# Transposed attention with paired 64-row score tiles, the mixer of one batch laid between the attention groups of the next, and transposes by DMA

## The chip, the cores and the metric

The kernel runs on one NeuronCore of a Trainium2 chip. Five engines work side by side, each through its own instructions in order: TensorE (PE in the profile; its weight loads have a row of their own, PEld), VectorE (DVE), ScalarE (ACT), GpSimd (POOL) and SyncE (SP). POOL and SP here mostly issue DMA transfers; those that change the type from float32 to bfloat16 are issued by POOL, stores by SP. TensorE writes to PSUM, eight banks of 512 float32 per partition; DVE and ACT read it.

The metric is the device time of one execution in microseconds. Lower is better.

## What is computed

The inputs `u` and `v` are 8 x 3008 x 256, `z` is 8 x 3008 x 64, all float32. For each of the 8 batches:

```python
scores = (z @ z.T) / 3008                     # 3008 x 3008
attn   = maximum(scores, 0) ** 2
x      = u * (attn @ v)                       # 3008 x 256, gated attention
h      = maximum(x.T @ w_tok1, 0) @ w_tok2    # token layers: 3008 -> 256 -> 3008
y      = x + h.T
h2     = maximum(y @ w_ch1, 0) @ w_ch2        # channel layers: 256 -> 1536 -> 256
out    = y + h2
```

The scores are symmetric, so a tile of them can serve as its own transpose. There is no softmax: squares of the positive scores multiply `v` directly.

## The kernel before

All matmuls take bfloat16 operands. The 3008 rows are cut into 24 tiles of 128 (the last holds 64 rows and is padded with zeros). The batches run one after another, and each goes through these stages.

**z transposes.** 24 tiles of `z` are transposed on TensorE (line 125) and copied by ACT to `z_T` (line 126), 64 partitions by 3072.

**Attention.** Queries are taken in six groups of 512 columns. For each of the 24 key tiles, one matmul with 64 contraction rows gives the scores of 128 keys by 512 queries (line 143). ACT applies relu and the scale (line 150), DVE squares (line 153), and four matmuls use the four 128-column pieces of the square as weights and the 256 columns of `v` as the moving operand (line 156), which accumulate the output with queries on partitions. Two PSUM banks hold the four accumulators. At the end of a query group DVE multiplies by `u` (line 165), which gives `x_sb` with rows on partitions.

**Token layers.** The first accumulates over the 24 row tiles into one bank (line 173), ACT applies relu (line 182); the second makes one 128 x 256 tile per row tile (line 187), which DVE adds to `x_sb` (line 193).

**Transposes.** The channel layers need `x_sb` with channels on partitions: 48 transposes of 128 x 128 on TensorE (line 199), copied by ACT and DVE in turn (lines 203 and 205).

**Channel layers.** For each 512 rows, twelve pairs of matmuls give the 1536 hidden channels (line 215); relu alternates between ACT and DVE (lines 222 and 224). Then each 128 rows take twelve matmuls of 256 columns (line 230), DVE adds `x_sb` (line 237), and SP stores the rows.

The order on each engine is made by the framework's scheduler from the order of the code and the free buffers: six PSUM buffers are shared by all tiles but the accumulators, and six work buffers hold relus and squares. It runs up to six score matmuls ahead of the matmuls that use them. POOL issues the loads of the next batch while one is worked on.

Of the kernel before, what the change touches and what calls it, by code (L numbers as in the profile page):

```python
# [8 lines left out]
F32 = mybir.dt.float32  # L10
BF16 = mybir.dt.bfloat16
AX = mybir.AluOpType
ACT = mybir.ActivationFunctionType


@with_exitstack
def kernel(
# [16 lines left out]

    P = 128
    KT = (S + P - 1) // P
    Sp = KT * P
    assert D == 256
    assert d_tok == 256
    assert d_ch % P == 0  # L40
    CHT = d_ch // P
    DT = D // P

    Q_SUB = 4
    QG = (KT + Q_SUB - 1) // Q_SUB
    Q_W = Q_SUB * P

# [3 lines left out]
    inbuf = ctx.enter_context(tc.tile_pool(name="inbuf", bufs=2))  # L51
    work = ctx.enter_context(tc.tile_pool(name="work", bufs=6))
    big = ctx.enter_context(tc.tile_pool(name="big", bufs=1))
    psum = ctx.enter_context(tc.tile_pool(name="psum", bufs=6, space=bass.MemoryType.PSUM))
    psum_acc = ctx.enter_context(tc.tile_pool(name="psum_acc", bufs=1, space=bass.MemoryType.PSUM))

    ident = consts.tile([P, P], BF16)
    make_identity(nc, ident)

    def load_sbuf_SD(ap_src, name):  # L60
        t = inbuf.tile([P, KT, D], BF16, tag=name, name=name)
        nc.gpsimd.memset(t[:, KT - 1, :], 0.0)
        nc.gpsimd.dma_start(
            out=t[:, : KT - 1, :],
            in_=ap_src[: (KT - 1) * P, :].rearrange("(t p) d -> p t d", p=P),
        )
        nc.gpsimd.dma_start(
            out=t[: S - (KT - 1) * P, KT - 1, :],
            in_=ap_src[(KT - 1) * P :, :],
        )  # L70
        return t

    def load_batch(b):
        z_sb = inbuf.tile([P, KT, d_qk], BF16, tag="z_sb")
        nc.gpsimd.memset(z_sb[:, KT - 1, :], 0.0)
        nc.gpsimd.dma_start(
            out=z_sb[:, : KT - 1, :],
            in_=z[b, : (KT - 1) * P, :].rearrange("(t p) d -> p t d", p=P),
        )
        nc.gpsimd.dma_start(  # L80
            out=z_sb[: S - (KT - 1) * P, KT - 1, :],
            in_=z[b, (KT - 1) * P :, :],
        )
        v_sb = load_sbuf_SD(v[b], "v_sb")
        u_sb = load_sbuf_SD(u[b], "u_sb")
        return z_sb, v_sb, u_sb

    next_data = load_batch(0)

    w_tok1_sb = consts.tile([P, KT, d_tok], BF16)  # L90
    nc.gpsimd.memset(w_tok1_sb[:, KT - 1, :], 0.0)
    nc.gpsimd.dma_start(
        out=w_tok1_sb[:, : KT - 1, :],
        in_=moe_w_tok1[: (KT - 1) * P, :].rearrange("(t p) d -> p t d", p=P),
    )
    nc.gpsimd.dma_start(
        out=w_tok1_sb[: S - (KT - 1) * P, KT - 1, :],
        in_=moe_w_tok1[(KT - 1) * P :, :],
    )

    w_tok2_sb = consts.tile([P, DT, Sp], BF16)
    nc.gpsimd.memset(w_tok2_sb[:, :, S:], 0.0)
    nc.gpsimd.dma_start(
        out=w_tok2_sb[:, :, :S],
        in_=moe_w_tok2.rearrange("(tc t) s -> t tc s", t=P),
    )

    w_ch1_sb = consts.tile([P, DT, d_ch], BF16)
    nc.gpsimd.dma_start(
        out=w_ch1_sb[:],  # L110
        in_=moe_w_ch1.rearrange("(dc d) c -> d dc c", d=P),
    )

    w_ch2_sb = consts.tile([P, CHT, D], BF16)
    nc.gpsimd.dma_start(
        out=w_ch2_sb[:],
        in_=moe_w_ch2.rearrange("(cc c) d -> c cc d", c=P),
    )

    for b in range(B):  # L120
        z_sb, v_sb, u_sb = next_data
        z_T = inbuf.tile([d_qk, Sp], BF16, tag="z_T")
        for k in range(KT):
            zt_ps = psum.tile([d_qk, P], BF16, tag="ps", name="zt_ps")
            nc.tensor.transpose(zt_ps[:], z_sb[:, k, :], ident)  # L125
            nc.scalar.copy(z_T[:, k * P:(k + 1) * P], zt_ps[:])  # L126
        if b + 1 < B:
            next_data = load_batch(b + 1)

        x_sb = big.tile([P, KT, D], BF16, tag="x_sb")  # L130

        for qg in range(QG):
            q0 = qg * Q_SUB
            n_q = min(Q_SUB, KT - q0)
            out_bank = [
                psum_acc.tile([P, 2, D], F32, tag=f"acc{i}", name=f"out_bank{i}")
                for i in range((n_q + 1) // 2)
            ]
            out_ps = [out_bank[i // 2][:, i % 2, :] for i in range(n_q)]
            qslice = slice(q0 * P, q0 * P + n_q * P)  # L140
            for k in range(KT):
                sc_ps = psum.tile([P, Q_W], F32, tag="ps", name="sc_ps")
                nc.tensor.matmul(  # L143
                    sc_ps[:, : n_q * P],
                    z_T[:, k * P : (k + 1) * P],
                    z_T[:, qslice],
                    start=True, stop=True,
                )
                relu_sb = work.tile([P, Q_W], BF16, tag="relu_sb")
                nc.scalar.activation(relu_sb[:, : n_q * P], sc_ps[:, : n_q * P],  # L150
                                     ACT.Relu, scale=inv_S)
                attn_sb = work.tile([P, Q_W], BF16, tag="attn_sb")
                nc.vector.tensor_mul(attn_sb[:, : n_q * P], relu_sb[:, : n_q * P],  # L153
                                     relu_sb[:, : n_q * P])
                for qi in range(n_q):
                    nc.tensor.matmul(  # L156
                        out_ps[qi][:],
                        attn_sb[:, qi * P : (qi + 1) * P],
                        v_sb[:, k, :],
                        start=(k == 0 and qi % 2 == 0),  # L160
                        stop=(k == KT - 1),
                        skip_group_check=True,
                    )
            for qi in range(n_q):
                nc.vector.tensor_mul(  # L165
                    x_sb[:, q0 + qi, :], u_sb[:, q0 + qi, :], out_ps[qi][:]
                )

        a_bank = psum_acc.tile([P, 2, D], F32, tag="acc0", name="a_bank")
        a_ps = [a_bank[:, i, :] for i in range(DT)]  # L170
        for k in range(KT):
            for tc_ in range(DT):
                nc.tensor.matmul(  # L173
                    a_ps[tc_][:],
                    w_tok1_sb[:, k, tc_ * P:(tc_ + 1) * P],
                    x_sb[:, k, :],
                    start=(k == 0 and tc_ == 0), stop=(k == KT - 1),
                    skip_group_check=True,
                )
        a_relu = work.tile([P, DT, D], BF16, tag="a_relu")  # L180
        for tc_ in range(DT):
            nc.scalar.activation(a_relu[:, tc_, :], a_ps[tc_][:], ACT.Relu)  # L182

        for k in range(KT):
            h_ps = psum.tile([P, D], F32, tag="ps", name="h_ps")
            for tc_ in range(DT):
                nc.tensor.matmul(  # L187
                    h_ps[:],
                    w_tok2_sb[:, tc_, k * P:(k + 1) * P],
                    a_relu[:, tc_, :],  # L190
                    start=(tc_ == 0), stop=(tc_ == DT - 1),
                )
            nc.vector.tensor_add(x_sb[:, k, :], x_sb[:, k, :], h_ps[:])  # L193

        u2T_all = big.tile([P, DT, Sp], BF16, tag="u2T_all")
        for k in range(KT):
            for dc in range(DT):
                t_ps = psum.tile([P, P], BF16, tag="ps", name="t_ps")
                nc.tensor.transpose(  # L199
                    t_ps[:], x_sb[:, k, dc * P:(dc + 1) * P], ident  # L200
                )
                if (k * DT + dc) % 2 == 0:
                    nc.scalar.copy(u2T_all[:, dc, k * P:(k + 1) * P], t_ps[:])  # L203
                else:
                    nc.vector.tensor_copy(u2T_all[:, dc, k * P:(k + 1) * P], t_ps[:])
        for sg in range(QG):
            s0 = sg * Q_SUB
            n_s = min(Q_SUB, KT - s0)
            SW = n_s * P
            u2T = u2T_all[:, :, s0 * P: s0 * P + SW]  # L210
            h2pre = big.tile([P, CHT, Q_W], BF16, tag="h2pre", bufs=2)
            for cc in range(CHT):
                hp = psum.tile([P, Q_W], F32, tag="ps", name="hp")
                for dc in range(DT):
                    nc.tensor.matmul(  # L215
                        hp[:, :SW],
                        w_ch1_sb[:, dc, cc * P:(cc + 1) * P],
                        u2T[:, dc, :],
                        start=(dc == 0), stop=(dc == DT - 1),
                    )  # L220
# [50 lines left out]
```

## Time and profile before

| | |
|---|---|
| runs | 1598.85 us median of 3 (1594.77 to 1600.70) |
| profiled execution, first to last instruction | 1595.4 us |
| median of the runs less that span | 3.45 us |
| TensorE matmul busy | 1539.8 us, 97% |
| DVE busy | 915.5 us, 57% |
| ACT busy | 837.8 us, 53% |
| POOL busy | 60.5 us, 4% |
| mean granted TensorE clock | 0.977 |

The profile comes from one execution. Its own time is given by the span from the first to the last instruction; the runs are timed from outside, without a profile. A row of a group reads: line, engine, operation, output and input tiles, shapes, count, then busy time and mean duration in ns, then the idle time of the engine just before these instructions and what ended it. A row of a stretch reads: from and to, length, then for each engine its busy time and number of instructions, then granted clock (1.00 is full), DMA share and GB/s. A row of the timeline reads: start, duration, engine, line, operation and the number of instructions merged in it. A row of a DMA issue ends with KB and the us from issue to landing.

The ends of matmuls are modelled by the profiler, and a matmul's duration contains its latency, so the pace of matmuls is read from one start to the next.

### The profile page before, as it was taken

Reading aid. Unit: us, or ns where it says so; the run is one execution under the profiler, and the core shown is the slowest. Engines: PE = TensorE matmul, PEld = TensorE weight load, DVE = VectorE, ACT = ScalarE, POOL = GpSimd, SP = SyncE. Lnnn points to the kernel's source line nnn. Section 1 sums busy time; section 2 is a strip of 40 time slices with the busy share of each in tenths; the row PEclk is TensorE's granted clock in tenths of the full one; section 3 lists DMA queues with packets and bytes.
Section 4 is the critical chain, followed back from the end, with each engine's and each line's share of the span. In section 5 each row is a group of like instructions: output and inputs, shape, how many; then the busy total and the mean of one; then the engine's idle time right before and its main releaser. Section 6 shows DMA issues by size and latency. Waiting matters only on the chain.

```text
span 1595.4 us, 27271 instructions
## 1 busy us (share of the span) xinstructions
PE 1539.8 (97%) x10512; PEld 954.0 (60%) x10560; DVE 915.5 (57%) x2208; ACT 837.8 (53%) x1841; POOL 60.5 (4%) x85
## 2 busy tenths in 40 slices
PE   7999999999999999999999999999999999999999
PEld 4556655566555665556655566555665556655566
DVE  3566555565565555556556565565655646556465
ACT  5663366633666336653367533775337743376442
POOL 4001000010000000010000100001000000000000
PEclk9999999999999899999999999999999999999999
DMA  9906110061100611006110051101510000100001
GB/s 176 126 1 91 54 22 1 1 92 54 23 1 1 95 50 23 1 6 93 48 21 1 10 92 50 17 1 18 88 50 3 1 1 27 52 1 1 1 28 52
DMA packets 105362, 58.77 MB, mean 37 GB/s; under 512 B 27984, under 2 KB 104720, under 8 KB 105232
## 3 DMA queue, kind: packets, MB, share of 16 engines
q0 software_dynamic: 78096, 32.38, 16.4%
q1 hardware_dynamic: 27136, 24.65, 4.6%
q8 instruction: 82, 1.34, 0.3%
q14 instruction: 48, 0.39, 0.1%
HBM read 64.75 MB, written 24.64 MB: 56 GB/s over the span
## 4 chain that ended last, share of the span: by engine, by line
PE 81%; ACT 8%; DVE 8%; issue 2%; DMA 1%; POOL 0%; POOLq 0%
PE out_bank L156 36%; PE op L230 16%; PE hp L215 16%; PE sc_ps L143 7%; ACT relu_sb L150 6%; DVE attn_sb L153 4%; PE a_bank L173 3%; DVE x_sb L193 3%; PE t_ps L199 3%; ACT z_T L126 2%; DMA v_sb<-in_v_dram 1%; ACT u2T_all L203 1%; DVE x_sb L165 0%; PE h_ps L187 0%; ACT a_relu L182 0%
## 5 line engine op out<-in xcount | busy, mean ns | idle before, releaser
L150 ACT ACTIVATE relu_sb<-sc_ps 128x512 bf16<-128x512 f32 x1152 | 582.6, 629 | 273.7 <-PE sc_ps L143 273.6
L153 DVE TENSOR_TENSOR attn_sb<-relu_sb 128x512 bf16<-128x512 bf16 x1152 | 466.1, 424 | 377.1 <-ACT relu_sb L150 333.2
L156 PE MATMUL out_bank<-v_sb,attn_sb 128*128 128x256 bf16 x4608 | 579.0, 275 | 20.1 <-DVE attn_sb L153 9.2
L156 PEld LDWEIGHTS <-attn_sb 128*128 128x128 bf16 x4608 | 387.7, 98 | 253.0 <-DVE attn_sb L153 180.6
L222 ACT ACTIVATE h2pre<-hp 128x512 bf16<-128x512 f32 x288 | 171.9, 597 | 290.8 <-DVE res L237 178.1
L143 PE MATMUL sc_ps<-z_T 64*128 64x512 bf16 x1152 | 295.3, 380 | 0.0
L230 PE MATMUL op<-w_ch_sb,h2pre 128*128 128x256 bf16 x2304 | 259.4, 273 | 0.0
L215 PE MATMUL hp<-u2T_all,w_ch_sb 128*128 128x512 bf16 x1104 | 251.0, 382 | 3.7 <-issue 1.5
L230 PEld LDWEIGHTS <-h2pre 128*128 128x128 bf16 x2304 | 225.5, 98 | 36.3
L224 DVE TENSOR_SCALAR h2pre<-hp 128x512 bf16<-128x512 f32 x288 | 199.3, 692 | 68.2 <-PE hp L215 65.0
L215 PEld LDWEIGHTS <-w_ch_sb 128*128 128x128 bf16 x1152 | 113.8, 99 | 128.9 <-issue 5.8
L143 PEld LDWEIGHTS <-z_T 64*128 64x128 bf16 x1152 | 91.3, 94 | 136.8 <-issue 55.7
L237 DVE TENSOR_TENSOR res<-op,x_sb 128x256 f32<-128x256 f32 x192 | 81.6, 425 | 157.1 <-PE op L230 157.1
L193 DVE TENSOR_TENSOR x_sb<-x_sb,h_ps 128x256 bf16<-128x256 bf16 x192 | 64.3, 415 | 56.7 <-PE h_ps L187 56.7
L203 ACT COPY u2T_all<-t_ps 128x128 bf16<-128x128 bf16 x192 | 46.3, 267 | 74.6 <-PE t_ps L199 69.4
L165 DVE TENSOR_TENSOR x_sb<-u_sb,out_bank 128x256 bf16<-128x256 bf16 x192 | 67.9, 416 | 3.9 <-PE out_bank L156 3.9
L199 PE MATMUL t_ps<-ident,x_sb 128*128 128x128 bf16 x384 | 53.1, 273 | 11.5 <-ACT u2T_all L203 9.3
L187 PE MATMUL h_ps<-a_relu,w_tok_sb 128*128 128x256 bf16 x384 | 56.9, 270 | 3.8 <-ACT a_relu L182 3.8
L173 PE MATMUL a_bank<-x_sb,w_tok_sb 128*128 128x256 bf16 x384 | 52.7, 307 | 5.0 <-DVE x_sb L165 5.0
L126 ACT COPY z_T<-zt_ps 64x128 bf16<-64x128 bf16 x192 | 32.1, 319 | 42.4 <-PE zt_ps L125 42.4
L199 PEld LDWEIGHTS <-x_sb 128*128 128x128 bf16 x384 | 38.1, 120 | 26.2 <-issue 21.4
L173 PEld LDWEIGHTS <-w_tok_sb 128*128 128x128 bf16 x384 | 42.3, 110 | 15.4 <-issue 6.4
(28 smaller groups left out, 193.4 us busy)
## 6 DMA issues: line engine op xcount, KB each, us to landing
out_dram<-res SPq DMA_DIRECT2D x184, 128.0 KB, 1.7
v_sb<-in_v_dram POOLq DMA_DIRECT2D x8, 1472.0 KB, 12.5
u_sb<-in_u_dram POOLq DMA_DIRECT2D x8, 1472.0 KB, 18.0
z_sb<-in_z_dram POOLq DMA_DIRECT2D x8, 368.0 KB, 6.0
w_ch_sb<-in_moe_w_ch_dram POOLq DMA_DIRECT2D x2, 768.0 KB, 30.9
w_tok_sb<-in_moe_w_tok_dram POOLq DMA_DIRECT2D x1, 1504.0 KB, 28.1
w_tok_sb<-in_moe_w_tok_dram POOLq DMA_DIRECT2D x1, 1472.0 KB, 23.0
out_dram<-res SPq DMA_DIRECT2D x8, 64.0 KB, 1.9
```

The source lines that it names most:

```text
L143: nc.tensor.matmul(sc_ps[:, : n_q * P], z_T[:, k * P : (k + 1) * P], z_T[:, qslice], start=True, stop=True,)
L150: nc.scalar.activation(relu_sb[:, : n_q * P], sc_ps[:, : n_q * P], ACT.Relu, scale=inv_S)
L153: nc.vector.tensor_mul(attn_sb[:, : n_q * P], relu_sb[:, : n_q * P], relu_sb[:, : n_q * P])
L156: nc.tensor.matmul(out_ps[qi][:], attn_sb[:, qi * P : (qi + 1) * P], v_sb[:, k, :], start=(k == 0 and qi % 2 == 0), stop=(k == KT - 1), sk ...
L173: nc.tensor.matmul(a_ps[tc_][:], w_tok1_sb[:, k, tc_ * P:(tc_ + 1) * P], x_sb[:, k, :], start=(k == 0 and tc_ == 0), stop=(k == KT - 1), s ...
L193: nc.vector.tensor_add(x_sb[:, k, :], x_sb[:, k, :], h_ps[:])
L199: nc.tensor.transpose(t_ps[:], x_sb[:, k, dc * P:(dc + 1) * P], ident)
L215: nc.tensor.matmul(hp[:, :SW], w_ch1_sb[:, dc, cc * P:(cc + 1) * P], u2T[:, dc, :], start=(dc == 0), stop=(dc == DT - 1),)
L222: nc.scalar.activation(h2pre[:, cc, :SW], hp[:, :SW], ACT.Relu)
L224: nc.vector.tensor_single_scalar(h2pre[:, cc, :SW], hp[:, :SW], 0.0, AX.max)
L230: nc.tensor.matmul(op[:], h2pre[:, cc, si * P:(si + 1) * P], w_ch2_sb[:, cc, :], start=(cc == 0), stop=(cc == CHT - 1),)
L237: nc.vector.tensor_add(res[:], op[:], x_sb[:, k, :])
```

## The change

The kernel is written anew around the same mathematics; nothing of the computation is left out.

- **Transposed attention.** `v` is now the weight operand and the square of the scores is the moving operand, so the attention output has channels on partitions: per key tile two matmuls of 512 columns instead of four of 256. The gate multiplies by a transposed `u`, and gives `xT`.
- **Paired scores.** `z` is loaded twice side by side, so that its transpose has the 64 rows on partitions 0 to 63 and again on 64 to 127. Two key tiles form a pair, one on each half of the rows, each into its own PSUM bank; one relu and one square serve both (1024 columns). Four key tiles form a group, six groups a strip of 512 queries, 36 groups a batch; the sixth strip is 448 wide, without padding. The last key tile, with 64 rows, is split over the halves in the same way.
- **DMA transposes.** `z`, `u`, the gated `xT` and `xT` after the token layers are transposed by DMA, issued by SP, instead of on TensorE.
- **Order by hand.** The order of the code is the order on each engine. The scores of a group, with their relus and squares, are issued one group ahead. The mixer (token and channel layers) of a batch is cut into pieces with a cost and an earliest group; after each key tile of the next batch's attention a running budget takes pieces from the queue. What is left after the last group runs at the end. A planner by accumulated load chooses ACT or DVE for the relus of the first channel layer.
- **PSUM.** Scores: two buffers of two banks; the accumulator: one buffer of two banks; all of the mixer: two buffers of one bank.

```diff
+    def load_z(b):
+        zr = sb.tile([P, KT, 2, d_qk], BF16, tag="zr", name="zr", bufs=1)
+        for h in range(2):
+            nc.gpsimd.dma_start(
+                out=zr[:, : KT - 1, h, :],
+                in_=z[b, : (KT - 1) * P, :].rearrange("(t p) d -> p t d", p=P))
...
+        zT = sb.tile([P, KT, P], BF16, tag="zT", name="zT", bufs=2)
+        nc.sync.dma_start_transpose(out=zT[:], in_=zr.rearrange("p t h d -> p (t h d)"))
...
+    def scores(n):
...
+        for pr in range(GK // 2):
+            sc = psum.tile([P, 2, QW], F32, tag="sc", name="sc", bufs=2)
+            for r in range(2):
+                k = g * GK + pr * 2 + r
+                h = slice(r * d_qk, (r + 1) * d_qk)
                 nc.tensor.matmul(
+                    sc[:, r, :W], zT[h, k * P:(k + 1) * P], zT[h, q * QW:q * QW + W],
+                    start=True, stop=True)
+            pss.append(sc)
+        for sc in pss:
+            rl = sb.tile([P, 2, QW], BF16, tag="rl", name="rl", bufs=3)
+            nc.scalar.activation(rl[:, :, :W], sc[:, :, :W], ACT.Relu, scale=inv_S)
+            at = sb.tile([P, 2, QW], BF16, tag="at", name="at", bufs=5)
+            nc.vector.tensor_mul(at[:, :, :W], rl[:, :, :W], rl[:, :, :W])
...
+    def av(n):
...
+            accs[b, q] = psum.tile([P, DT, QW], F32, tag="acc", name="acc", bufs=1)
...
+                nc.tensor.matmul(
+                    acc[:, dh, :W], vt[rows, k, dh * P:(dh + 1) * P], at[rows],
+                    start=(k == 0), stop=(g == NG - 1 and last), skip_group_check=True)
...
+    def gate(b, q):
...
+        x = sb.tile([P, DT, QW // P, P], BF16, tag="x", name="x_sb", bufs=7)
+        nc.sync.dma_start_transpose(
+            out=x.rearrange("p h t d -> p (h t) d"), in_=xT.rearrange("p h s -> p (h s)"))
...
+    def relu_out(dst, src, n):
+        if load["ACT"] + 0.1 + n / 1200 <= load["DVE"] + 0.15 + n / 960:
+            load["ACT"] += 0.1 + n / 1200
+            nc.scalar.activation(dst, src, ACT.Relu)
+        else:
+            load["DVE"] += 0.15 + n / 960
+            nc.vector.tensor_single_scalar(dst, src, 0.0, AX.max)
...
+        def tok2(q, dh):
...
+            h = psum.tile([P, QW], F32, tag="mm", name="h_ps", bufs=2)
...
+            nc.vector.tensor_add(xT[:, dh, :W], xT[:, dh, :W], h[:, :W])
...
+        def ch1(q, cc):
...
+            hp = psum.tile([P, QW], F32, tag="mm", name="hp", bufs=2)
...
+        def ch2(q, half):
+            op = psum.tile([P, 2, D], F32, tag="mm", name="op", bufs=2)
...
+            res = sb.tile([P, 2, D], F32, tag="res", name="res", bufs=3)
...
+            head.append(Work(0.87, g0, lambda q=q: tok1(q)))
...
+                head.append(Work(0.43, g0 + 4, lambda q=q, dh=dh: tok2(q, dh)))
+        c1 = [[Work(0.43, g0 + 6, lambda q=q, cc=cc: ch1(q, cc)) for cc in range(CHT)]
+              for q in range(NQ)]
+        c2 = [[Work(2.7, g0 + 6, lambda q=q, hf=hf: ch2(q, hf)) for hf in range(2)]
+              for q in range(NQ)]
...
+    share = per_batch / (NQ * NG)
...
+    for n in range(N):
...
+        if n + 1 < N:
+            scores(n + 1)
+        if b >= 1:
+            budget += share
+        thunks = av(n)
+        for j, t in enumerate(thunks):
+            t()
+            if j == GK - 1 and g == NG - 1:
+                gate(b, q)
+            want = budget * (GK - 1 - j) / GK
+            while budget > want:
+                i = next((i for i, w in enumerate(queue) if w.earliest <= n), None)
...
+                w.fn()
+                budget -= w.cost
+        if q == NQ - 1 and g == NG - 1:
+            head, tail = mixer(b, n + 3)
+            queue = head + queue + tail
+    for w in queue:
+        w.fn()
```

More of the change, by code (lines that the diff above doesn't have):

```diff
@@ new lines, in load_v @@
+    def load_v(b, parts):
+        vt = sb.tile([P, KT, D], BF16, tag="v", name="v_sb", bufs=2)
+        step = (KT - 1 + parts - 1) // parts
+        for t0 in range(0, KT - 1, step):
+            t1 = min(t0 + step, KT - 1)
+            nc.gpsimd.dma_start(
+                out=vt[:, t0:t1, :],
+                in_=v[b, t0 * P:t1 * P, :].rearrange("(t p) d -> p t d", p=P))
+        for r in range(2):
+            nc.gpsimd.dma_start(
+                out=vt[r * TAIL:(r + 1) * TAIL, KT - 1, :], in_=v[b, (KT - 1) * P:, :])
+        return vt
@@ L120 @@
[L120 to L186, printed above, removed]
-                nc.tensor.matmul(
[L188 to L220, printed above, removed]
-                if cc % 2 == 0:
-                    nc.scalar.activation(h2pre[:, cc, :SW], hp[:, :SW], ACT.Relu)
-                else:
-                    nc.vector.tensor_single_scalar(h2pre[:, cc, :SW], hp[:, :SW],
-                                                   0.0, AX.max)
-            for si in range(n_s):
-                k = s0 + si
-                op = psum.tile([P, D], F32, tag="ps", name="op")
@@ new lines, in av, with one @@
+    def av(n):
+        b, q, g = groups[n]
+        W = widths[q]
+        if g == 0:
+            accs[b, q] = psum.tile([P, DT, QW], F32, tag="acc", name="acc", bufs=1)
+        acc = accs[b, q]
+        tiles = attn.pop(n)
+        vt = vs[b]
+        order = list(range(GK))
+        if g == NG - 1:
+            order = [GK - 1] + order[:-1]
+        def one(i, last):
+            k = g * GK + i
+            at = tiles[i // 2][:, i % 2, :W]
+            for dh in range(DT):
+                rows = slice(0, P)
+                if k == KT - 1:
+                    rows = slice(dh * TAIL, (dh + 1) * TAIL)
+                nc.tensor.matmul(
+                    acc[:, dh, :W], vt[rows, k, dh * P:(dh + 1) * P], at[rows],
+                    start=(k == 0), stop=(g == NG - 1 and last), skip_group_check=True)
+        return [lambda i=i, j=j: one(i, j == GK - 1) for j, i in enumerate(order)]
@@ new lines, in ch2 @@
+            load["DVE"] += 0.7
+        for q in range(NQ):
+            head.append(Work(0.87, g0, lambda q=q: tok1(q)))
+        for q in range(NQ):
+            for dh in range(DT):
+                head.append(Work(0.43, g0 + 4, lambda q=q, dh=dh: tok2(q, dh)))
[3 more added lines that the diff above has]
+              for q in range(NQ)]
@@ new lines, in mixer @@
+        tail += c1[0]
+        for q in range(NQ):
+            nxt = c1[q + 1] if q + 1 < NQ else []
+            half = len(nxt) // 2
+            tail += nxt[:half] + [c2[q][0]] + nxt[half:] + [c2[q][1]]
+        return head, tail
+    zTs[0] = load_z(0)
+    vs[0] = load_v(0, 4)
+    uTs[0, 0] = load_uT(0, 0)
+    load_weights()
+    uTs[0, 1] = load_uT(0, 1)
+    queue = []
+    per_batch = 0.87 * NQ + 0.43 * NQ * DT + 0.43 * CHT * NQ + 2.7 * 2 * NQ
+    share = per_batch / (NQ * NG)
+    budget = 0.0
```

230 lines of the change are left out of this document (155 added, 75 removed).

## The prediction, made before the change was run

> **What bounds the kernel now.** I read the page's engine shares and its chain of waits first, then the stretches of one batch (the second, from 211.19 us on), then the groups of instructions by shape, then single rows of the timeline.
>
> ```profile
> span 1595.4 us, 27271 instructions
> PE 1539.8 (97%) x10512; PEld 954.0 (60%) x10560; DVE 915.5 (57%) x2208; ACT 837.8 (53%) x1841; POOL 60.5 (4%) x85
> PE 81%; ACT 8%; DVE 8%; issue 2%; DMA 1%; POOL 0%; POOLq 0%
> ```
>
> TensorE is busy 97% of the span and carries 81% of the chain; ACT and DVE are half idle. The next view gives busy time by stage: attention, token layer 1, token layer 2, the transposes, the channel layers, the z transposes of the next batch.
>
> ```profile
> 211.19:319.95 108.76, 105.69 (x721) 59.69 (x721) 65.76 (x167) 73.39 (x149) 2.79 (x5) 1.00 0.06 5
> 319.95:325.82 5.87, 5.40 (x48) 4.69 (x48) 0.61 (x2) 0.43 (x2) 4.07 (x5) 1.00 0.78 98
> 325.82:332.89 7.07, 7.07 (x48) 4.62 (x48) 6.43 (x20) 0.23 (x1) 0.00 (x0) 1.00 1.42 193
> 332.89:340.78 7.89, 6.47 (x50) 4.77 (x48) 6.13 (x27) 5.41 (x23) 0.00 (x0) 0.66 1.09 148
> 340.78:404.09 63.31, 62.83 (x429) 42.38 (x433) 35.14 (x62) 21.91 (x38) 0.00 (x0) 0.99 0.14 46
> 404.09:407.61 3.52, 3.40 (x25) 2.25 (x25) 0.42 (x1) 3.24 (x21) 0.00 (x0) 1.00 0.20 60
> ```
>
> One batch is 196.4 us. To see whether "busy" is really full, I take the pace from starts: 23 channel matmuls of 512 columns, 48 of 256, and so on; then an attention stretch with short runs of each kind.
>
> ```profile
> 352.11 5.13 PE L215 MATMUL hp<-u2T_all,w_ch_sb 128*128 128x512 bf16 x23
> 357.07 5.40 PE L230 MATMUL op<-w_ch_sb,h2pre 128*128 128x256 bf16 x48
> 362.53 0.38 PE L215 MATMUL hp<-u2T_all,w_ch_sb 128*128 128x512 bf16 x1
> ...
> 70.20 0.61 PE L156 MATMUL out_bank<-v_sb,attn_sb 128*128 128x256 bf16 x4
> 70.74 1.03 PE L143 MATMUL sc_ps<-z_T 64*128 64x512 bf16 x4
> 71.71 0.39 PE L156 MATMUL out_bank<-v_sb,attn_sb 128*128 128x256 bf16 x2
> ```
>
> (357.07 - 352.11)/23 = 0.2157 us for 512 columns. From 357.07 to 362.53 are 5.46 us: 48 of 256 columns and one 512 whose record is missing (23 of 24), so (5.46 - 0.216)/48 = 0.1092 us. A 64-row score costs the same as a 128-row matmul. Each change between 64-row and 128-row work costs 0.10: 0.54 - 4 x 0.1092 = 0.103, and 0.97 - 4 x 0.2157 = 0.107. By these prices the attention of a batch is 144 x (0.2157 + 4 x 0.1092) = 94.0; the other 14.8 of 108.8 are changes and waits for the score chain.
>
> **The change, part by part.** Every step is costed on TensorE, then I look for what makes it wait. "Group" is four key tiles of one 512-query strip; 36 groups make a batch.
>
> *Attention matmuls.* A group has two score pairs (0.431 if the two halves of a pair run at once), eight attention-times-V matmuls of 512 columns (1.726) and two changes (0.20): 2.36 us. 36 groups are 85.0; the sixth strip is 448 wide, less 6 x 2.157/8 = 1.6: 83.4. Nothing in the trace shows two 64-row matmuls on different rows. The bounds for a pair are 0.2157 (both at once) and 0.431 (one after another); I take the first, because the two use different rows and different PSUM banks, and the nearest row, a full 128-row matmul, streams exactly those rows in 0.2157. The other end adds 36 x 2 x 0.2157 x 8, less a 48th, = 122 us.
>
> [...]
>
> *Removed on TensorE.* z transposes (3.5) and the transposes before the channel layers (7.9) go to DMA. Padding 3072 to 3008 is in the strip width above.
>
> *Mixer matmuls.* Token 1: 48 x 0.1092 = 5.2. Token 2, now 24 of 512: 5.2. Channel 1: 144 x 0.2157 = 31.1. Channel 2: 288 x 0.1092 = 31.4. Less 0.8 for the narrow strip: 72.2 a batch.
>
> Now the waits. ACT and DVE serve the new, longer tiles at these prices:
>
> ```profile
> L150 ACT ACTIVATE relu_sb<-sc_ps 128x512 bf16<-128x512 f32 x1152 | 582.6, 629 | 273.7 <-PE sc_ps L143 273.6
> L153 DVE TENSOR_TENSOR attn_sb<-relu_sb 128x512 bf16<-128x512 bf16 x1152 | 466.1, 424 | 377.1 <-ACT relu_sb L150 333.2 <-PE out_bank L156 2.5
> L224 DVE TENSOR_SCALAR h2pre<-hp 128x512 bf16<-128x512 f32 x288 | 199.3, 692 | 68.2 <-PE hp L215 65.0
> L222 ACT ACTIVATE h2pre<-hp 128x512 bf16<-128x512 f32 x288 | 171.9, 597 | 290.8 <-DVE res L237 178.1 <-PE hp L215 107.6 <-PE t_ps L199 5.1
> L165 DVE TENSOR_TENSOR x_sb<-u_sb,out_bank 128x256 bf16<-128x256 bf16 x192 | 67.9, 416 | 3.9 <-PE out_bank L156 3.9
> L182 ACT ACTIVATE a_relu<-a_bank 128x256 bf16<-128x256 f32 x16 | 5.3, 381 | 67.0 <-PE a_bank L173 67.0
> ...
> 909.58 0.39 PE L143 MATMUL sc_ps<-z_T 64*128 64x512 bf16 x1
> 910.00 0.60 ACT L150 ACTIVATE relu_sb<-sc_ps 128x512 bf16<-128x512 f32 x1 [1.48 <-PE sc_ps L143]
> 910.63 0.43 DVE L153 TENSOR_TENSOR attn_sb<-relu_sb 128x512 bf16<-128x512 bf16 x1 [1.65 <-ACT relu_sb L150]
> 911.11 0.61 PE L156 MATMUL out_bank<-v_sb,attn_sb 128*128 128x256 bf16 x4 [1.15 <-DVE attn_sb L153]
> ```
>
> ACT takes 216 ns for 256 more columns (597 - 381), so 629 + 2 x 216 = 1.06 us for 1024; the next one overlaps it by 0.12 (629 against 582.6/1152 = 506). DVE from PSUM takes 276 ns more per 256 (692 - 416): 1.24 for the 1024 of a gate. The square of 1024 lies between 0.42 and 0.85; I take 0.75. A score matmul that starts at t reaches ACT at t + 0.42.
>
> *The evacuation queue.* In a group that starts at T, ACT and DVE are given the two relus and two squares of the next group before anything of the mixer. The first relu starts at about T + 0.5, the second ends at T + 2.5, the second square at T + 3.3. Mixer evacuations stand behind them, and the mixer has two PSUM buffers. TensorE: scores to 0.53, AV 0.96, two channel matmul pairs 1.82, AV 2.25; the third pair needs the first one's buffer, free at 2.5 + 0.6 = 3.1 (ACT) or 3.3 + 0.7 = 4.0 (DVE). The planner's own balance (0.53 a piece on ACT, 0.68 on DVE, 0.7 more on DVE for each channel-2 half) puts 48 of 72 on ACT; so, and with less where an AV lies between, that is about 0.9 us in each group with three or more of them. Following the budget (2.05 a group, pieces of 0.43 and 2.7) by hand, five groups in ten are such, and ten hold 24 of the 72 pieces: 15 groups x 0.9 = 13.5. Token 2 evacuates only by DVE: 1.75 x 2.5 groups = 4.4. Together 17.9 a batch, bounded by 0 and by twice that.
>
> *The gate.* The accumulator has one buffer, so the next strip's first AV waits 0.20 + 1.24 + 0.05 after the last one where it would have come after 0.53: 0.95 a strip, 5.7 a batch.
>
> *Clock.* Pauses can cost more than themselves. Token 1 ran twice as follows; the first row is the pause before the slow one.
>
> ```profile
> 909.60:912.35 2.75, 0.98 (x6) 0.47 (x6) 1.23 (x4) 0.60 (x1) 0.43 (x2) 0.97 0.00 0
> 912.35:919.30 6.95, 6.95 (x48) 5.52 (x48) 0.61 (x2) 0.00 (x0) 4.27 (x5) 0.76 0.87 107
> 319.95:325.35 5.40, 5.40 (x48) 4.69 (x48) 0.61 (x2) 0.00 (x0) 4.07 (x5) 1.00 0.74 93
> ```
>
> After 2.75 us with 0.98 busy, the granted clock was 0.76 and the same work took 1.55 us more. The new waits are 1 to 2 us between long busy runs, so I take zero; at worst one such loss a strip, 48 x 1.55 = 74 us.
>
> *DMA transposes.* Per batch: gate to x (6), token 2 to its row form (6), u (6), each 256 KB, and z with 768 KB: 21 units of 256 KB, all issued by SP beside the output stores.
>
> ```profile
> q0 software_dynamic: 78096, 32.38, 16.4%
> q1 hardware_dynamic: 27136, 24.65, 4.6%
> ...
> out_dram<-res SPq DMA_DIRECT2D x184, 128.0 KB, 1.7
> z_sb<-in_z_dram POOLq DMA_DIRECT2D x8, 368.0 KB, 6.0
> z_sb<-in_z_dram POOLq DMA_DIRECT2D x8, 8.0 KB, 4.6
> ```
>
> No transpose by DMA is in the trace. Lower bound: the store's 1.7 us. For the upper one, packets: 16.4% of 16 x 1595.4 us over 78,096 is 53.6 ns each (415 B), 4.6% over 27,136 is 43.3 ns (908 B). In packets of a 128-element line, 256 B, a unit is 1024 x 53.6/16 = 3.4 us; in 64 B packets 4096 x 43.3/16 = 11.1. I take 3.4, the nearest in packet size: 72 us of SP's queue a batch, behind 179 us of TensorE, and every consumer comes at least three groups later. SP is passed in order: a u transpose waits for its load, and stores stand behind it, but `res` has three buffers and channel 2 makes 12 of them in a batch, one each 15 us. So zero; the cover is gone when a unit takes over 179/21 = 8.5 us.
>
> *Start and end.* The first z loads of before were issued by POOL like this:
>
> ```profile
> 1.30 1.61 POOL L76 DMA_DIRECT2D z_sb<-in_z_dram  x1 [0.27 <-issue]
> ...
> 3.23 0.58 POOL L80 DMA_DIRECT2D z_sb<-in_z_dram  x1
> ```
>
> Now z comes in six: 1.3 + 2 x 1.61 + 3 x 0.58, the last is issued at about 6.3 us and lands 4.6 later, and its transpose takes 3 units, 10.2: first score at 21 us. The last batch's mixer has no attention beside it: token 1 5.2, its relu 1, token 2 at the DVE's pace 12 x 0.74 = 8.9, channel 1 at two buffers' pace (0.43 + 0.20 + 0.64 + 0.05)/2 = 0.66 x 72 = 47.5, channel 2 31.4, the last store 2.6: 97.
>
> *Sum.* Start 21; first batch, attention alone, 83.4 + 5.7 = 89; seven batches of 89.1 + 72.2 + 17.9 = 179.2, together 1254; end 97. Span 1461 against 1595.4. The runs' median, 1598.85, is 3.5 above the span: **1464 us**.
>
> **The rivals.**
> 1. *The evacuations are hidden after all.* For: ACT has room, with two relus (2.0) and 48 x 0.6/36 = 0.8 of the mixer in a group of 5 us. Against: their order is fixed, relus first. 1464 - 7 x 17.9 - 16 at the end = 1323.
> 2. *A pair runs one after the other*, so the change doesn't do what it says. For: 64-row scores now show 0.2157 each. Against: all of them use the same rows. 1464 + 122 = 1586, hardly faster.
> 3. *The transposes set the pace: slower.* One mechanism: SP issues them in order, x and the row form come out of it, and TensorE waits for both. It decides from 8.5 us a unit. At 11.1 it is 233 us a batch, 8 x 233 + 20 = 1884. For: nothing here shows that they move in long packets. Against: 256 B lines are the layout on both sides.
>
> [...]
>
> **How the numbers follow.** Forecast 0.60 (1390 to 1530), hidden evacuations 0.14, serial pairs 0.13, transposes 0.13. The range 1310 to 1600 takes in the forecast with half or double its waits and the clock's loss, most of rivals 1 and 2, and leaves out rival 3 and the edges, some 0.2. Half a percent is what a measurement of this kernel can tell from no change. Slower has rival 3 and the last of rival 2: 0.14; within it 0.02; faster 0.84.
>
> **What would show it.** Score pairs: starts of the two halves together, pairs 0.22 apart. Evacuations: TensorE idle before channel 1 with ACT or DVE as releaser, about 18 us a batch. Gate: about 0.95 idle before the first AV of a strip. Transposes: landing under 5 us and no idle of TensorE ended by DMA after the start. The forecast is wrong if a group without mixer takes more than 2.6 us, if DMA ends TensorE's waits, or if the granted clock sits below 0.95 in the middle.

## The result, and the profile after

The changed kernel takes 1467.29 us (median of 4 runs, 1466.61 to 1468.50) against 1598.57 for the kernel before: ratio 0.918, 95% interval 0.9167 to 0.9193. The profiled execution spans 1465.4 us; the prediction had 1461 for it.

First the page of the changed kernel: engine shares and the chain of waits.

```profile
span 1465.4 us, 18578 instructions
PE 1296.3 (88%) x7488; PEld 630.6 (43%) x7488; DVE 700.0 (48%) x1028; ACT 760.6 (52%) x965; POOL 126.9 (9%) x178
PE 60%; ACT 13%; DVE 11%; issue 10%; DMA 5%; POOL 0%; ACTq 0%; DVEq 0%; SPq 0%; POOLq 0%
```

TensorE went from 97% busy to 88%, and its part of the chain from 81% to 60%. It has much less to do, and now it waits. The next view gives busy time by stretch: the third batch's attention with the second batch's mixer between, the mixer of the last batch alone, and the first batch's attention alone.

```profile
303.47:481.18 177.71, 160.85 (x936) 78.65 (x937) 87.10 (x129) 95.20 (x122) 15.23 (x22) 1.00 0.44 71
1367.57:1465.40 97.83, 81.96 (x506) 48.96 (x504) 34.20 (x52) 27.26 (x48) 0.00 (x0) 0.99 0.20 51
28.75:121.00 92.25, 84.73 (x428) 30.57 (x429) 53.95 (x77) 68.40 (x72) 21.95 (x29) 1.00 1.18 147
```

A batch in the middle takes 177.7 us (196.4 before), and the granted clock is 1.00. Now what TensorE waited for, over the whole run: us in total, times, longest.

```profile
PE hp L257 <- ACT h2pre L209: 40.2, 94, 0.9
PE acc L177 <- DVE xT L191: 38.6, 40, 1.2
PE sc L145 <- DMA zT<-zr: 28.8, 1, 28.8
PE op L271 <- ACT h2pre L209: 12.0, 21, 0.7
PE hp L257 <- DVE h2pre L212: 11.6, 38, 0.4
PE acc L177 <- DVE xT L196: 10.4, 7, 1.5
PE h_ps L239 <- DVE xT L243: 9.1, 33, 0.5
...
PE a_ps L226 <- DMA x_sb<-xT: 2.1, 3, 1.0
```

Every large wait is one that the prediction named: evacuations of the mixer (L209, L212, L243), the gate (L191, L196) and the start. After the first z transpose, a DMA ends only three waits, 2.1 us together. Three rows of the timeline show a group without mixer:

```profile
52.80 0.60 PE L145 MATMUL sc<-zT 64*128 64x512 bf16 x4
53.34 1.90 PE L177 MATMUL acc<-at,v_sb 128*128 128x512 bf16 x8
55.17 0.60 PE L145 MATMUL sc<-zT 64*128 64x512 bf16 x4
```

Two pairs and one change take 0.54 (52.80 to 53.34), the group with both changes 2.37 (52.80 to 55.17; 2.36 was predicted). Within a pair, the second half starts 3 to 6 ns after the first, and the next pair 0.222 us after that. The wait before the third channel piece of a full group looks like this; the relus of the next group (two, 158.90) stand on ACT before the first evacuation (160.72):

```profile
158.90 1.94 ACT L151 ACTIVATE rl<-sc 128x1024 bf16<-128x1024 f32 x2 [0.43 <-PE sc L145]
159.44 1.03 PE L257 MATMUL hp<-xT,w_ch_sb 128*128 128x512 bf16 x4
160.72 0.60 ACT L209 ACTIVATE h2pre<-hp 128x512 bf16<-128x512 f32 x1
161.38 0.59 PE L257 MATMUL hp<-xT,w_ch_sb 128*128 128x512 bf16 x2 [0.91 <-ACT h2pre L209]
```

Last the DMA queues, and the issues of the transposes with the median time to landing.

```profile
q1 hardware_dynamic: 202624, 68.71, 23.0%
q0 software_dynamic: 105360, 35.86, 22.6%
...
uT<-ur SPq DMA_TRANSPOSE x48, 3.1
x_sb<-xT SPq DMA_TRANSPOSE x48, 3.2
u_sb<-xT SPq DMA_TRANSPOSE x48, 3.3
zT<-zr SPq DMA_TRANSPOSE x8, 5.7
```

Less the stores of before (27,136 packets, 24.65 MB), the transposes are 175,488 packets for 44.06 MB: 251 bytes each. The time of their packets, 23.0% of 16 x 1465.4 less the stores' 4.6% of 16 x 1595.4, is 24 ns a packet: a unit of 256 KB costs the 16 engines 1.54 us by its packets' time and lands in 3.2.

### The profile page after: what moved, and what is told of

Its sections match the earlier page's. It is cut to its first block, busy times and chain, and to the rows that moved or that the text cites. A ratio compares the mean times of both kernels' runs of the same rounds, so it can differ in the third digit from the quotient of the medians.

```text
span 1465.4 us, 18578 instructions
## 1 busy us (share of the span) xinstructions
PE 1296.3 (88%) x7488; PEld 630.6 (43%) x7488; DVE 700.0 (48%) x1028; ACT 760.6 (52%) x965; POOL 126.9 (9%) x178
## 3 DMA queue, kind: packets, MB, share of 16 engines
q0 software_dynamic: 105360, 35.86, 22.6%
## 4 chain that ended last, share of the span: by engine, by line
PE 60%; ACT 13%; DVE 11%; issue 10%; DMA 5%; POOL 0%; ACTq 0%; DVEq 0%; SPq 0%; POOLq 0%
PE acc L177 22%; PE op L271 18%; PE hp L257 11%; ACT rl L151 9%; PE sc L145 6%; ACT h2pre L209 4%; DVE xT L191 3%; DMA x_sb<-xT 3%; DVE at L153 3%; DVE h2pre L212 2%; DVE xT L243 2%; PE h_ps L239 2%; PE a_ps L226 1%; DMA zT<-zr 1%; DVE res L277 0%
## 5 line engine op out<-in xcount | busy, mean ns | idle before, releaser
L151 ACT ACTIVATE rl<-sc 128x1024 bf16<-128x1024 f32 (+1 forms) x576 | 547.9, 1003 | 488.6 <-PE sc L145 487.8
L177 PE MATMUL acc<-at,v_sb 128*128 128x512 bf16 (+2 forms) x2304 | 593.0, 376 | 52.5 <-DVE xT L191 38.6
L153 DVE TENSOR_TENSOR at<-rl 128x1024 bf16<-128x1024 bf16 (+1 forms) x576 | 391.6, 681 | 462.9 <-ACT rl L151 461.9
L257 PE MATMUL hp<-xT,w_ch_sb 128*128 128x512 bf16 (+1 forms) x1152 | 318.7, 374 | 56.6 <-ACT h2pre L209 40.2
L177 PEld LDWEIGHTS <-v_sb 128*128 128x128 bf16 (+1 forms) x2304 | 203.3, 97 | 337.3 <-issue 162.6
L209 ACT ACTIVATE h2pre<-hp 128x512 bf16<-128x512 f32 (+1 forms) x380 | 217.7, 592 | 155.9 <-PE hp L257 154.3
L271 PE MATMUL op<-w_ch_sb,h2pre 128*128 128x256 bf16 (+1 forms) x2304 | 267.7, 273 | 13.5 <-ACT h2pre L209 12.0
L271 PEld LDWEIGHTS <-h2pre 128*128 128x128 bf16 (+1 forms) x2304 | 225.6, 98 | 64.0 <-issue 23.6
L145 PE MATMUL sc<-zT 64*128 64x512 bf16 (+1 forms) x1152 | 173.9, 378 | 30.1 <-DMA zT<-zr 28.8
L212 DVE TENSOR_SCALAR h2pre<-hp 128x512 bf16<-128x512 f32 (+1 forms) x196 | 132.7, 679 | 112.2 <-PE hp L257 111.5
L243 DVE TENSOR_TENSOR xT<-xT,h_ps 128x512 bf16<-128x512 bf16 (+1 forms) x96 | 61.1, 674 | 9.2 <-PE h_ps L239 6.9
L239 PE MATMUL h_ps<-w_tok_sb,a_sb 128*128 128x512 bf16 (+1 forms) x192 | 54.1, 373 | 10.4 <-DVE xT L243 9.1
L191 DVE TENSOR_TENSOR xT<-acc,uT 128x1024 bf16<-128x1024 f32 (+1 forms) x48 | 56.5, 1176 | 7.4 <-PE acc L177 7.4
```

The lines of the kernel that those rows point to most:

```text
L145: nc.tensor.matmul(sc[:, r, :W], zT[h, k * P:(k + 1) * P], zT[h, q * QW:q * QW + W], start=True, stop=True)
L151: nc.scalar.activation(rl[:, :, :W], sc[:, :, :W], ACT.Relu, scale=inv_S)
L153: nc.vector.tensor_mul(at[:, :, :W], rl[:, :, :W], rl[:, :, :W])
L177: nc.tensor.matmul(acc[:, dh, :W], vt[rows, k, dh * P:(dh + 1) * P], at[rows], start=(k == 0), stop=(g == NG - 1 and last), skip_group_che ...
L191: nc.vector.tensor_mul(xT[:, :, :full * P].rearrange("p h (t s) -> p h t s", s=P), acc[:, :, :full * P].rearrange("p h (t s) -> p h t s", ...
L209: nc.scalar.activation(dst, src, ACT.Relu)
```

## The experiments

All are variants of the changed kernel, compared with its 1467.29 us. The first four ask whether the sum's terms are what they seem.

**Both halves of a pair on the same rows.**

```diff
-                h = slice(r * d_qk, (r + 1) * d_qk)
+                h = slice(0, d_qk)
```

> Both halves of a score pair use rows 0 to 63, nothing else changes. Theory (the two halves run at once in the changed kernel, starts 3 to 5 ns apart, and TensorE is the bound): a pair costs 0.431 us instead of 0.216, the start and every evacuation chain shift with it, so the waits stay: 288 groups x 0.431 less 2.6 for the narrow strips = 122 us more, 1589 us. Rival (part of the scores' time was waiting for ACT and DVE anyway): the rise is absorbed, under 60 us, below 1527.

Measured: 1543.76 us, 76 more. In its timeline the four scores and the change take 0.97 in place of 0.54:

```profile
53.94 1.03 PE L145 MATMUL sc<-zT 64*128 64x512 bf16 x4
54.91 1.41 PEld L177 LDWEIGHTS <-v_sb 128*128 128x128 bf16 x8 [0.42 <-issue]
...
PE hp L257 <- ACT h2pre L209: 30.6, 94, 0.7
PE acc L177 <- DVE xT L191: 22.0, 40, 0.9
```

So the two halves do run at once, and undoing that costs 0.43 a group; but only 76 of the 122 us reach the end. The rest came out of waits: the gate's wait fell by 0.4 each time (its end does not depend on the scores, and the scores now fill part of it), and the evacuations' waits fell too. The likely reason, not tried by itself, is that the first relu starts after the first pair, 0.216 later, while TensorE itself comes 0.43 later. In the waits view 36 of the 46 us are gone. The expectation had let the waits stay; that was wrong. Neither side's number was met, the mechanism was.

**The second relu and square later.** `scores(n + 1)` issues its four matmuls and the first relu and square; the second pair's follow after the pieces of the first key tile.

```diff
-        if n + 1 < N:
-            scores(n + 1)
+        late = scores(n + 1) if n + 1 < N else None
...
+            if j == 0 and late is not None:
+                late()
```

> The relu and square of the second score pair of the next group are issued after the first key tile's mixer pieces instead of before them; the same instructions. Theory (mixer evacuations wait in ACT's and DVE's order behind both relus and squares; the profile shows 10.0 us before channel 1 and 2.7 before channel 2 a batch): an evacuation on ACT starts at T + 1.6 instead of T + 2.5, so about 8 of the 12.7 us go, 7 x 8 = 56 less: 1411 us. Rival (two PSUM buffers are simply too few, whatever the order): within 10 us of 1467. Second rival: the late square delays the next group's attention-times-V: slower than 1467.

Measured: 1446.46 us, 21 less, not 56. The order does hold the evacuations up, since nothing else was changed, but more than half of the waits stayed:

```profile
PE hp L260 <- ACT h2pre L212: 23.5, 72, 0.8
PE hp L260 <- DVE h2pre L215: 13.4, 40, 0.4
```

**Mixer pieces ahead of the first matmul of a strip.**

```diff
         for j, t in enumerate(thunks):
+            if g == 0 and j == 0:
+                want = budget * (GK - 1) / GK
+                while budget > want:
...
             t()
```

> At the first group of a strip, the first share of mixer pieces is issued before the first attention-times-V matmul instead of after it. Theory (TensorE waits 1.2 us there for the gate to read the one accumulator, 7.5 us a batch): two pieces of 0.43 cover most of it wherever the queue has pieces, five strips of six in seven batches: 7 x 5 x 0.9 = 32 us less, 1435 us. Rival (the evacuations of those pieces then queue behind the gate on DVE, so the wait moves to the next piece): less than 10 us gained.

Measured: 1460.67 us, 7 less: the rival's number. The wait for the gate did shrink, from 38.6 + 10.4 to 9.7 + 10.4, but it came back before token 2 and channel 1, whose evacuations now stand behind the gate on DVE or wait for ACT:

```profile
PE acc L177 <- DVE xT L191: 9.7, 19, 1.2
PE h_ps L239 <- DVE xT L243: 18.9, 23, 2.2
PE hp L257 <- ACT h2pre L209: 44.3, 99, 0.9
```

The clock took some of it too: of the seven waits of 2.17 us that this run has before token 2, four are followed by about 3.4 us at little over half the granted clock, as in this row (0.54). Ten matmuls of 0.2157 us would take 2.2 there, so the four cost an estimated 5 us. The changed kernel has no such stretch between its first and its last matmuls: there the clock reads 1.00.

```profile
1208.20:1211.60 3.40, 3.39 (x10) 1.04 (x9) 2.57 (x5) 0.00 (x0) 0.00 (x0) 0.54 0.49 94
```

**Nothing laid between.** The mixer of a batch is issued whole after its attention.

```diff
             head, tail = mixer(b, n + 3)
-            queue = head + queue + tail
+            for w in head + tail:
+                w.fn()
```

> The mixer of each batch is issued whole right after its attention, nothing is laid between groups. Theory (TensorE is full in both, and laying the mixer between only trades waits of one kind for another): per batch 90 us of attention as in the first batch plus 95 of mixer as at the end: 32 + 8 x 185 = 1512 us, 45 more. Rival (laying between is what hides ACT and DVE, so without it their time shows): over 1600 us.

Measured: 1574.42 us, 107 more, between both. Neither side had one wait: token 1 needs the last strip's x, and in six batches that transpose takes some 10 us to land. The next load of v starts at the same moment; both follow the batch's last attention-times-V.

```profile
124.42 3.36 POOL L88 DMA_DIRECT2D v_sb<-in_v_dram  x4 [6.94 <-PE acc L177]
...
125.99 1.61 SPq L199 DMA_TRANSPOSE x_sb<-xT  x1
...
136.30 1.87 PE L226 MATMUL a_ps<-x_sb,w_tok_sb 128*128 128x256 bf16 x8 [7.82 <-DMA x_sb<-xT]
```

While TensorE waits, the granted clock falls to half and stays there for some 10 us, into token 2 (first row below). The other two rows go from token 1 of one batch to token 1 of the next, once with the late transpose and once, at the end, where no load is issued beside it: there x lands in 3.1 us and the clock is 1.00.

```profile
132.10:142.40 10.30, 5.19 (x15) 2.10 (x16) 2.06 (x3) 0.60 (x1) 0.00 (x0) 0.51 0.74 99
318.40:512.85 194.45, 167.69 (x926) 80.17 (x936) 87.98 (x129) 97.37 (x122) 15.24 (x21) 0.97 0.40 65
1289.93:1475.37 185.44, 163.03 (x921) 79.34 (x932) 87.00 (x127) 95.48 (x120) 2.50 (x5) 1.00 0.19 43
```

So laying the mixer between groups is worth 107 us: about half of it (six times 9.0) by covering a late DMA transpose with the low clock behind it, half (seven times 185.4 less 177.7) by covering evacuations and the starts of the stages. That the load of v is what delays the transpose was not tried by itself.

The next three ask what the DMA transposes cost.

**Mixer weights later.** `load_weights()` is moved from the start to the fourth group.

> The four mixer weight loads are issued at the fourth group instead of before the first; they are first used in the second batch. Theory (the transpose of z took 18.6 us from issue to landing at the start and 5.7 in the middle because it shares the DMA engines with the loads): the first score starts at about 20 us instead of 28.75, the rest is unchanged, 9 us less: 1458. Rival (the first transpose is slow for another reason, or waits for v's load, which stays): first score within 2 us of 28.75, time within 3 of 1467.

Measured: 1465.38 us, 2 less. The rival, nearly: the first score starts at 26.55 instead of 28.75, so the weights were not the main thing that made the first transpose late.

```profile
26.55 1.03 PE L145 MATMUL sc<-zT 64*128 64x512 bf16 x4 [26.55 <-DMA zT<-zr]
```

**Each transpose of 256 KB five times, and nine times.**

```diff
+    def again(src):
+        for i in range(4):        # 8 in the second
+            spare = sb.tile([P, QW // P * DT, P], BF16, tag="spare", name="spare", bufs=2)
+            nc.sync.dma_start_transpose(out=spare[:], in_=src)
```

> Each of the 18 transposes of 256 KB in a batch is issued four times more, into a spare tile that nobody reads. Theory (SP and the DMA engines have room behind TensorE; a unit costs SP 1.25 us and the engines 1024 packets x 24.6 ns / 16 = 1.57): 93 units are 146 us of the engines and 116 of SP in a batch of 178, so the time rises by less than 15 us, to 1467 to 1482. Rival (the cover is thin: the landing of a unit, 3.2 us, is what counts in the queue, and 93 x 3.2 = 298 is over 178): over 2000 us.

> The same with eight more copies of each. Theory: 165 units of 1.57 us are 259 us of the DMA engines a batch against 178 of TensorE, so now they set the pace: 7 to 8 x 259 and the start and end, 2000 to 2200 us. Rival (the engines overlap transposes better than the packet times say): under 1600.

Measured: 1597.51 us with four copies (130 more) and 2481.02 with eight (1014 more). The queues of the one and of the other:

```profile
q1 hardware_dynamic: 810880, 219.78, 76.4%
q0 software_dynamic: 105360, 35.86, 21.5%
```

```profile
q1 hardware_dynamic: 1419136, 370.85, 82.1%
q0 software_dynamic: 105360, 35.86, 14.4%
```

The price was right, by the packets' time: from one copy to five, the hardware queue grows by 0.764 x 1597.6 - 0.230 x 1465.4 = 884 us of all 16 engines for 576 units, 1.53 each. The conclusion for five was wrong. 93 units are 143 us a batch, under 178; but the loads take another 22.6% of the engines (40 us) and the stores 9, and 192 is over 178. The two queues' packets take 97.9% of the span. With nine, 165 units are 252 us, with loads and stores (40 + 9) 301 a batch, eight batches 2410; with start and end that is about what came. The expectation had left loads and stores out again.

That the engines were full is argued, not shown. The share adds up the times that packets took, and it can pass 1: 1.38 in a stretch of the run with four copies. And the copies load SP as well: it issues them in order, into two spare buffers, and by its waits view (last two rows) it waits for these to be free for 204 us in that run and 481 in the one with eight. Two buffers and 3.2 us to landing allow an estimated one unit in 1.6 us, nearly the price of 1.53, so these two runs do not tell SP's queue from the engines.

```profile
540.00:560.00 20.00, 18.54 (x126) 10.32 (x124) 9.47 (x14) 10.01 (x14) 3.05 (x4) 1.00 1.38 159
...
SPq L117 <- DMA spare<-xT: 149.2, 122, 5.5
...
SPq L117 <- DMA spare<-ur: 55.1, 57, 4.8
```

The last four put the waits together again.

**Late square, and pieces evenly.** A piece is taken only while more than half of it is due, measured from the budget at the group's start.

```diff
-            want = budget * (GK - 1 - j) / GK
-            while budget > want:
+            want = whole * (GK - 1 - j) / GK
+            while True:
...
+                if i is None or budget - queue[i].cost / 2 <= want:
+                    break
```

> The late second relu and square (1446 us alone), and the budget spends the mixer pieces evenly over the four key tiles (about one each) where before it took two, two, one, none. Theory (what is left of the waits, 47 us in all before channel 1, channel 2 and token 2, comes from pieces issued in pairs into two PSUM buffers): with an attention-times-V pair between any two pieces the first buffer is free in time, and 30 of the 47 go: 1416 us. Rival (the second relu of 1.02 us on ACT and the squares on DVE still stand before half of the evacuations): less than 10 us gained, over 1436.

Measured: 1413.92 us, 53 less than the changed kernel and the time that was expected; its place was met in part. Booked over the whole run from start to start, as in the table below, the waits before channel 2 fall from 19.0 us to 1.0 and those before channel 1 from 88.0 to 63.7: 42 of the 53 us. Some 7 more go before attention-times-V. Of the 33 us gained on the late square alone, 19 lie before channel 1, channel 2 and token 2, where 30 were expected (that run's missing matmul records put in from the order, which is the same). So pieces in pairs into two buffers were only part of what was left: channel 1 still waits 6.7 us a batch (10.0 in the changed kernel).

**The gate in halves.** The accumulator is two tiles of a bank each, the gate one multiplication for each; the first group of a strip does two key tiles of the first half, then of the second.

```diff
-            accs[b, q] = psum.tile([P, DT, QW], F32, tag="acc", name="acc", bufs=1)
+            accs[b, q] = [psum.tile([P, QW], F32, tag=f"acc{i}", name=f"acc{i}", bufs=1)
+                          for i in range(DT)]
```

> The accumulator is two tiles of one bank, the gate two multiplications of 512 columns, and the first group of a strip does both key tiles of its first half before the second half. Nothing else against the changed kernel. Theory (TensorE waits 1.2 us a strip for the 1.22 us gate to leave the one accumulator, 7.5 us a batch): the first half is free after 0.69 instead of 1.22, the second half's wait is covered by 0.43 of matmuls, so about 0.6 a strip go, 48 x 0.6 = 29 less: 1438 us. Rival (as in the run that laid pieces before the first matmul, DVE is then behind and the wait comes back before token 2 and channel 1): less than 10 us gained.

Measured: 1447.35 us, 20 less; 29 were expected. The gate's waits fell by that 29 (49.0 to 19.9), and 9 came back, before token 2 (9.1 to 12.8), before token 1 (2.1 to 5.1) and in small parts before channel 1:

```profile
PE acc L178 <- DVE xT L199: 12.8, 23, 0.6
PE h_ps L247 <- DVE xT L251: 12.8, 33, 1.0
PE acc L178 <- DVE xT L204: 7.1, 7, 1.0
```

**Everything together, and a second time with the weights later.** Beside the two above: z and v of the first batch in three parts, a transpose for each; weights after the third group; in the last batch, every second channel-1 piece uses an idle score buffer. In the second run the weights come at group 21.

> The late second relu and square, the even budget (1414 us together), the gate in halves, z and v of the first batch in three parts with a transpose each, the mixer weights after the third group, and two more PSUM buffers for the first channel layer of the last batch, where the score banks are idle. Theory (the terms are separate waits of TensorE and add up): gate 25 less, start 12 less (first score at about 15 us instead of 28), end 15 less (17.4 us of waits before channel 1 there): 1414 - 52 = 1362 us. Rival (the first strip is then paced by the loads, and DVE by the gate, so half of it comes back): about 1390.

> As the run with everything together (1376 us), but the mixer weights are loaded at group 21 of the first batch, behind the loads of z, v and u that come up before it, instead of at group 3. Theory (there TensorE waited 8.6 us once for a gate whose transposed u stood in SP's queue behind the transpose of the next z, and that behind its load, and that behind the weights): this wait and the low clock after it go, nothing else changes: 1364 us. Rival (the loads of the next batch alone keep u back, weights or not): the wait stays, within 3 us of 1376.

Measured: 1376.37 us (1368.43 to 1386.39) and 1367.48 (1366.89 to 1368.13; ratio to the kernel before 0.8553, 0.8539 to 0.8568). In the first, TensorE waited once 8.47 us for a gate:

```profile
90.52 3.14 PE L181 MATMUL acc<-at,v_sb 128*128 128x512 bf16 x7 [8.47 <-DVE xT L202]
```

That wait is gone in the second run, and with it 9 us and the spread: the u transpose had stood in SP's queue behind the z transpose of the next batch, whose load the weights had delayed. From the even kernel to this one the span falls by 46: 12 at the start (first attention-times-V at 19.8 instead of 31.4), 18 between the first and the last, 16 at the end (82.4 instead of 98.3, with no wait left before channel 1). The gate was expected to give 25, the start 12 and the end 15, so the times, 1376 and 1367, came near the theory (1362, then 1364), with the gate's part too small. It is the fastest version of the study.

## Why the prediction was right

The booking behind this table goes from each matmul's start to the next one's: what exceeds 0.2157 us for 512 columns (a pair counted once), as much less for 448, or 0.1092 for 256 is a wait of the line that starts late. Up to 0.13 at each change between 64 and 128 rows is booked as change.

| step | predicted, us | measured, us |
|---|---|---|
| first score | 21 | 28.8 |
| first score to first attention-times-V | 0 | 3.2 |
| first batch | 89 | 93.0 |
| matmuls of a middle batch | 148.4 | 146.9 |
| changes of row count, a batch | 7.2 | 7.1 |
| evacuations, a batch | 17.9 | 15.3 |
| before attention-times-V, a batch (gate) | 5.7 | 7.4 (6.5) |
| seven batches | 1254 | 1242.6 |
| end | 97 | 97.8 |

**That the error is 0.2% is partly luck.** The start and the first batch were 15 us too short, the seven batches 11 too long. The steps themselves held:

- *Pairs at once.* Right: 0.226 from the start of a pair to the start of the next, and the same-rows run shows 0.43 more a group.
- *Matmuls.* 1.5 too many: the halves of the last key tile, 64 rows each, also run at once, which saves 6 x 0.2157 a batch and was not counted.
- *Evacuations.* Place and cause right: the even run takes away 42 us before channels 1 and 2 with the order alone. Token 2 was mis-sized: 2.6 instead of 4.4, the others 12.7 for 13.5.
- *Gate.* The cause is shown by the halves run. The size: 0.8 to 1.5 a strip instead of 0.95, 6.5 a batch. The 1.5 comes after the narrow strip, whose gate is two multiplications one after the other, which was not counted. The other 0.9 in the table are short waits elsewhere in the attention.
- *Clock.* Its loss was taken as zero, and it was: 1.00 over the span, with 1.5 us as the longest wait after the start. The margin is thin, as the run with pieces ahead shows with its waits of 2.17 us.
- *DMA transposes hidden.* Right but for three waits of 2.1 us together, and 256-byte packets were right (251 B). But the price of a unit was taken at 3.4 us of all engines and is 1.54; and the threshold, 8.5 us a unit, left out that loads and stores use the same engines: (178 - 40 - 9)/21 = 6.1 by packet times. The two errors went opposite ways. By the time of its packets, a transpose moves 251 B in 24 ns, 10 GB/s an engine; the stores of before, 908 B in 43.3 ns, have 21, and its loads, 415 B in 53.6 ns, 8.
- *Start.* Wrong: the z transpose was costed at three units, 10.2 us, and took 18.6 (it was issued at 10.14, the first score came at 28.75). In the middle of the run the same transpose lands in 5.7. Loads of v, u and the weights run beside it at the start; moving the weights away gave only 2 us, cutting z and v into parts 12. SP's waits put 8.6 us of the transpose on the load of v, but which of the loads does it was not tried by itself.

**The rivals.** Evacuations hidden after all (1323): no, not in this order; with the even order 15.3 us a batch become 9.2, so most of them stay even in the version of 1367. Serial pairs (1586): the run that makes them serial took 1544, so that rival was also overpriced, because waits absorb part of a longer step. Transposes setting the pace: no, but closer than the sum said: packets take 45.6% of the engines' time (23.0 + 22.6), and four more copies are enough to lose the whole gain.

## What to carry to other kernels

When work of two kinds shares in-order engines and few PSUM buffers, cost not only the matmuls but what stands ahead of each evacuation in its engine's queue; here two changes of order alone, with no work removed, were worth 53 us, and a cover that is laid over one wait can put the same wait one step later. A step made longer or shorter does not pass its whole difference on when there are waits behind it: 122 us of matmul time were 76 us of the kernel's. For transfers, add up all users of the DMA engines, and the engine that issues them in order, and ask whether each sum fits under the compute; the new transfers alone are not the sum.

## What the runs showed that was not expected

- A wait can cost more than itself. After four of seven waits of 2.17 us (pieces ahead of the first matmul) the granted clock was little over half (0.53 to 0.55) for 3.4 us, and with waits of 7.5 to 7.9 us (nothing laid between) for 10 us and more (0.51); the changed kernel's longest wait after the start, 1.5 us, left it at 1.00.
- A DMA transpose of 256 KB costs the engines 1.54 us and lands in 3.2 (median) in the changed kernel, but took some 10 us when a load of v started with it (nothing laid between; 10.5 to 11.5, six times, in the changed kernel), and the one of 768 KB 18.6 at the start against a median of 5.7.
- SP passes its queue in order: one z transpose that waits for its load stood there from 73.73 to 83.35 us, a u transpose came only behind it, at 83.46, and TensorE waited 8.5 us (the first of the two runs with everything).
- POOL runs ahead of the order of the code to the first blocked load: the load of v for a later batch starts at the moment when the attention that frees its buffer ends, beside the transpose that the mixer waits for next (nothing laid between: POOL issued the load at 124.42 us, after 6.94 us of waiting for attention-times-V, SP the transpose at 125.99).
